# Scores on half the array: a shared PSUM pool, 64-row score matmuls in pairs, and weights cast by DMA

## The chip, the cores and the metric

The kernel runs on one core of one Trainium2 chip. The metric is the device time of one execution in microseconds (us). Five engines of a core work side by side, each through its own queue in order: TensorE (PE, matrix multiply; loading its stationary operand is listed apart as PEld), VectorE (DVE), ScalarE (ACT), GpSimd (POOL) and SyncE (SP, which here only issues DMAs). Matrix products land in PSUM, eight banks of 128 partitions x 512 float32; everything else lives in SBUF, 128 partitions wide. A shape such as 128x448 is partitions x elements per partition.

## The reference

Attention for 8 batches of 12 heads over 448 positions of width 64, then a two-layer feed-forward over all 3584 tokens of width 768. All inputs and the output are float32.

```python
q_n, k_n = (rmsnorm(q, g_q), rmsnorm(k, g_k))      # x / sqrt(mean(x*x) + 1e-6) * g
scores = scale * np.matmul(q_n, k_n.transpose(0, 1, 3, 2))
attn = softmax(scores)
x = matmul(attn, v), heads side by side            # 3584 x 768
h = x @ w_in                                       # 768 x 2048
g = h * np.clip(h + 3.0, 0.0, 6.0) / 6.0
out = g @ w_out                                    # 2048 x 768
```

## The kernel before

**Pairs.** Two heads of one batch make a pair, since two heads of width 64 fill 128 partitions; there are 48 pairs, six per batch. The 448 positions are three blocks of 128 and a rest of 64. For k and v the rest of head 0 and the rest of head 1 are put together in one more block of 128, so a pair has seven key blocks: three of head 0, a mixed one, three of head 1.

**From input to scores.** `load_k`, `load_q` and `load_v` bring two pairs at a time (the first two pairs singly) into staging rings of three groups. `square` (POOL, early also ACT or DVE), `stats_sum` (DVE) and `stats_rstd` (ACT) give 1/rms; `normalize` multiplies it in and rounds to bf16. Then q and k are transposed so that the head width lies on the partitions. For pairs 0 to 13 TensorE does it (`transposes`), and `put_q` and `put_k` copy from PSUM; from pair 14 (`TD`) on a transposing DMA on SP's queue does it (`transposes_dma`), and `scale_q` applies g to q in place. Transposed q has head 0 on partitions 0 to 63 and head 1 on 64 to 127. So that one matmul on all 128 rows gives the scores of a single head, transposed k is kept padded: seven blocks, in which the other head's rows are zero (`clear_k`, `clear_kq`). `put_k` therefore copies in two halves, and the DMA transposes 11 blocks of 128 per pair.

**Scores, softmax, weighing.** `score` is one matmul of 128 rows and 448 columns per key block, into two PSUM banks in turn (`sc_r`). `expo` (ACT) takes the exponential into SBUF. `weigh` multiplies the exponentials by v with a column of ones, so that the row sum comes along; per pair 4 matmuls of 130 columns and 24 of 65, in two halves, into `av_ps` (two banks). `divide` (DVE) normalises, and x is transposed: on TensorE for pairs 0 to 13 (`x_out`, `put_x`), later by a transposing DMA (`x_out_dma`).

**Feed-forward.** `h_mm`: per batch 16 items of six matmuls of 448 columns, followed by `relu` (ACT) and `gate` (DVE). `y_mm`: per block of 128 tokens and half of the output columns, 16 matmuls of 384 columns, then `y_copy` and `y_store`. An item holds one bank from its first matmul to the end of `gate` or `y_copy`. It has three banks (`m_r`), and the two score banks too once all scores are done; the eighth bank (`t_ps`) belongs to the transposes.

**Weights.** Sixteen chunks of 768 KB are loaded by SP into three float32 buffers (`load_w`) and cast to bf16 by whichever of POOL, DVE and ACT the planner picks (`cast_w`). `W_AFTER` says after which group's v load a chunk may be issued.

**What sets the order.** No scheduler of the compiler: `Plan` is a list scheduler that runs while the program is built. Every operation has a key (smaller goes first), the engines that could do it with a planned duration each, and what it depends on. `Plan.run` walks through planned time and emits an instruction when its engine is free. TensorE's feed-forward items stand in two lanes, and a credit (`share`) divides TensorE between them and the attention. The planned durations decide only the order; on the chip every instruction waits for its semaphores.

Of the kernel before, what the change touches and what calls it, by code (L numbers as in the profile page):

```python
# [26 lines left out]
class Op:  # L27

    def __init__(self, key, ways, deps, lag, size):
        self.key, self.ways, self.lag, self.size = key, ways, lag, size
        self.deps = {id(d): d for d in deps if d is not None}
        self.next, self.end, self.time = [], None, 0.0
        for d in self.deps.values():
            d.next.append(self)
        self.left = len(self.deps)


class Item:
    def __init__(self, place):
        self.place, self.ops, self.bank, self.out = place, [], None, None


class Plan:

    HOP = 60
    PRICE, FAIR = {"POOL": 0.5, "ACT": 2.0, "DVE": 1.5}, 0
    ISSUE, LAND, RATE = 600, 1700, 270.0
    STEADY, SLACK = 110e3, 500

    def __init__(self, share):
        self.free = {e: 0.0 for e in ("PE", "ACT", "DVE", "POOL", "SP", "pipe")}
        self.known, self.todo = [], 0
        self.lanes, self.row, self.banks = {"h": [], "y": []}, [], []
        self.share, self.credit = share, 0.0  # L60

    def add(self, key, ways, deps=(), lag=0, size=0, hold=False):
        op = Op(key, ways, deps, lag, size)
# [6 lines left out]
    def dma(self, key, n, size, fn, deps=(), queue="SP", hold=False):  # L70

        return self.add(key, [(queue, self.ISSUE * n, fn)], deps, self.LAND, size, hold)
# [4 lines left out]
    def item(self, lane, place, count, ns, fn, deps):  # L77

        it = Item(place)
        it.ops = [Op(None, [("PE", ns, lambda i=i: fn(i, it.bank[0]))], deps if i == 0 else [], 165, 0)  # L80
                  for i in range(count)]
        self.lanes[lane].append(it)
        return it

    def next_item(self, now, soon):
        best = None
        for lane in self.lanes.values():
            if lane and lane[0].ops[0].left == 0 and (best is None or lane[0].place < best[0].place):
                free = [x for x in self.banks if x[1] is None or x[1].end is not None]
                bank = min(free, key=lambda x: x[1].end if x[1] else 0.0, default=None)  # L90
                if bank is None:
                    continue
                t = max(lane[0].ops[0].time, bank[1].end + self.HOP if bank[1] else 0.0)
                if t <= now:
                    best = (lane[0], bank)
                else:
                    soon.append(t)
        return best

    def begin(self, op, engine, ns, fn, now):  # L100
        fn()
        self.free[engine] = now + ns
        op.end = now + ns + op.lag
        if op.size:
            self.free["pipe"] = max(self.free["pipe"], now + self.ISSUE) + op.size / self.RATE
            op.end = max(op.end, self.free["pipe"] + op.lag)
# [8 lines left out]
    def run(self):  # L115
        now = 0.0
        while self.todo or self.row or any(self.lanes.values()):
            soon = [t for t in self.free.values() if t > now]
            best = {}
            for op in self.known:  # L120
                if op.time > now:
                    soon.append(op.time)
                    continue
                engine, ns, fn = min(op.ways, key=lambda w: max(self.free[w[0]], now) + w[1] * (
                    self.PRICE.get(w[0], 1.0) if op.key[0] >= self.FAIR else 1.0))
                if self.free[engine] <= now and (engine not in best or op.key < best[engine][0].key):
                    best[engine] = (op, ns, fn)
            if self.free["PE"] <= now and ("PE" not in best or self.credit < 0):
                if not self.row:
                    pick = self.next_item(now, soon)  # L130
                    if pick:
                        it, bank = pick
# [3 lines left out]
                        it.bank, bank[1] = bank, it.out  # L136
                        self.row = list(it.ops)
                if self.row:
                    best["PE"] = (self.row[0], *self.row[0].ways[0][1:])
            if not best:  # L140
                now = min(soon)
            for engine, (op, ns, fn) in best.items():
# [10 lines left out]
                self.begin(op, engine, ns, fn, now)  # L153
# [4 lines left out]
def kernel(  # L158
# [25 lines left out]
    NS = 3  # L184
    GP = 2
    NV, NK, NX, NE, NQ = 4, 3, 3, 14, 3
    WC = 256
    WR = 4
    NW = 3
# [16 lines left out]
    q_st = ring(NS, [P, GP, 2, 4, D], FP32, "q_st")  # L206
    k_st = ring(NS, [P, GP, 2, 5, D], FP32, "k_st")
    v_st = ring(NS, [P, GP, 2, 4, D], FP32, "v_st")
    vaug = ring(NV, [P, 4, 2, D + 1], BF16, "vaug")
    kq_r = ring(NK, [P, 11 * P], BF16, "kq")  # L210
    kpad = [x[:, 0:7 * P] for x in kq_r]
    sq_r = ring(2, [P, GP, 8, D], FP32, "sq")
    ssq_r = ring(2, [P, 2, GP, 8], FP32, "ssq")
    lnv_r = ring(2, [P, 2, GP, 8], FP32, "lnv")
    rstd_r = ring(2, [P, 2, GP, 8], FP32, "rstd")
    qk_r = ring(NQ, [P, 2, 4, 2, D], BF16, "qk")
    qT_r = [x[:, 7 * P:7 * P + S] for x in kq_r]
    eT_r = ring(NE, [P, W4], BF16, "eT")
# [4 lines left out]
    w_st = ring(NW, [P, NKT * WC], FP32, "w_st")  # L223

    KQ = 11 * P // 2
    kq_st = [w_st[i][:, 0:KQ].bitcast(BF16) for i in range(NQ)]
# [21 lines left out]
    def part_of(p, n):  # L248
        return (p // GP) % NS, slice(p % GP, p % GP + n)

    def blocks(src):
        return src[:, 0:FULL, :].rearrange("h (p t) d -> p h (t d)", t=NT)

    def load_q(eng, p, n):
        g, pr = part_of(p, n)
        src, dst = heads(q, p, n), q_st[g][:, pr].rearrange("p r h t d -> p (r h) t d")
        eng.dma_start(out=dst[:, :, 0:NT, :].rearrange("p h t d -> p h (t d)"), in_=blocks(src))
# [531 lines left out]
```

## Time and profile before

| | us |
|---|---|
| median of three timed runs | 449.7 (449.42 to 449.94) |
| span of the profiled execution, first to last instruction | 449.5 |
| TensorE busy | 424.5 |
| ACT, DVE, POOL busy | 274.8, 240.1, 229.7 |
| first TensorE matmul starts | 9.9 |
| TensorE busy in the stretch 30 to 60 us | 24.9 of 30 |
| TensorE busy in the stretch 300 to 350 us | 50.0 of 50 |

The page gives no time of its own for the profiled execution beside the span; 0.2 us lie between the span and the median.

How to read it: a line of a group says source line, engine, operation, written tile <- read tiles, shapes and count; then busy time and mean duration in ns; then how long the engine had stood idle just before, and what ended that. Matmuls overlap in the pipeline, so the durations of a group add up to more than the time that passed; the distance between starts is what one costs. The granted clock of TensorE was 0.94 from 30 to 60 us and 1.00 in the other stretches up to 400 us.

### The profile page before, as it was taken

The page shows a single profiled execution, that of the slowest core. Times are in us where ns is not written, and L with a number is a line of the kernel's source. Part 1 is how long each engine was busy: PE and PEld are TensorE (multiplying, and loading weights), DVE is VectorE, ACT ScalarE, POOL GpSimd, SP SyncE. Part 2 cuts the span into 40 slices and gives each one's busy share as a digit, 9 for nine tenths or more (in the row PEclk, how much of TensorE's full clock was granted, in tenths as well). Part 3 has the DMA queues.
Part 4 walks back from the last instruction along what each step waited for, and adds up shares of the span by engine and source line. Part 5 has one row for each costly group of instructions (what it writes and reads, how often), then busy time and mean ns, then how long its engine had stood idle before and what let it go on. Part 6 is the DMA issues. An engine that isn't in the chain of part 4 may idle for free.

```text
span 449.5 us, 9164 instructions
## 1 busy us (share of the span) xinstructions
PE 424.5 (94%) x3512; PEld 255.4 (57%) x3512; DVE 240.1 (53%) x428; ACT 274.8 (61%) x581; POOL 229.7 (51%) x251
## 2 busy tenths in 40 slices
PE   0888799899999989999999999999999999999996
PEld 0455366565566555666566565656565655555563
DVE  6899888845474346646444555453433253343321
ACT  2678678853487678878776777777767551132100
POOL 5899999958577766855667467552310000000000
PEclk9999899999999999999999999999999999999999
DMA  6899999981999999999899777955545210110021
GB/s 160 208 295 247 306 294 283 309 296 47 216 229 191 227 231 199 169 232 188 160 184 219 177 176 171 223 140 76 93 106 72 73 26 36 61 45 36 24 83 70
DMA packets 140908, 73.94 MB, mean 164 GB/s; under 512 B 90176, under 2 KB 137280, under 8 KB 140864
## 3 DMA queue, kind: packets, MB, share of 16 engines
q1 hardware_dynamic: 139232, 72.44, 69.3%
q10 hardware_dynamic: 1632, 0.92, 0.8%
q8 instruction: 27, 0.44, 0.4%
q14 instruction: 17, 0.14, 0.1%
HBM read 45.61 MB, written 11.01 MB: 126 GB/s over the span
## 4 chain that ended last, share of the span: by engine, by line
PE 84%; DMA 6%; POOL 2%; DVE 2%; ACT 2%; SPq 1%; issue 1%; POOLq 0%
PE m L461 29%; PE m L480 26%; PE sc L393 11%; PE av L419 7%; PE sc L480 5%; DMA k_st<-in_k_dram 4%; DMA kq<-w_st 3%; PE sc L461 3%; PE av L413 2%; ACT eT L399 2%; POOL qk L333 1%; POOL sq L315 1%; DVE vaug L280 1%; PE t_ps L349 1%; SPq L277 0%
## 5 line engine op out<-in xcount | busy, mean ns | idle before, releaser
L399 ACT ACTIVATE eT<-sc 128x448 bf16<-128x448 f32 x336 | 175.7, 542 | 48.6 <-PE sc L393 44.6
L461 PE MATMUL m<-xT,w_in_sb 128*128 128x448 bf16 x708 | 165.7, 355 | 0.2
L480 PE MATMUL m<-w_out_sb,gT 128*128 128x384 bf16 x768 | 150.0, 326 | 0.0
L393 PE MATMUL sc<-kq 128*128 128x448 bf16 x336 | 115.9, 359 | 8.2 <-ACT eT L399 6.4
L480 PEld LDWEIGHTS <-gT 128*128 128x128 bf16 x896 | 87.2, 98 | 62.3 <-issue 0.5
L461 PEld LDWEIGHTS <-w_in_sb 128*128 128x128 bf16 x768 | 74.1, 98 | 68.8 <-issue 6.0
L472 DVE SCALAR_TENSOR_TENSOR gT<-t_sb,m 128x448 bf16<-128x448 f32 x118 | 73.0, 620 | 72.9 <-ACT t_sb L467 72.4
L467 ACT ACTIVATE t_sb<-m 128x448 f32<-128x448 f32 x118 | 63.7, 541 | 47.3 <-PE m L461 44.3
L318 DVE TENSOR_REDUCE ssq<-sq 128x16 f32<-128x1024 f32 (+1 forms) x56 | 58.3, 1058 | 8.4 <-POOL sq L315 7.1
L359 POOL TENSOR_TENSOR w_st<-k_st,rstd 128x256 bf16<-128x256 f32 x68 | 40.2, 612 | 41.3 <-DMA kq<-w_st 40.6
L280 DVE COPY y_sb<-m 128x384 f32<-128x384 f32 x39 | 21.7, 557 | 61.4 <-PE m L480 61.2
L419 PE MATMUL av<-vaug,eT 128*128 128x65 bf16 x1152 | 54.5, 194 | 0.0
L419 PEld LDWEIGHTS <-eT 128*128 128x128 bf16 x1152 | 50.8, 99 | 4.4 <-issue 0.4
L315 POOL TENSOR_TENSOR sq<-k_st 128x1024 f32<-128x1024 f32 (+1 forms) x24 | 42.4, 1765 | 12.7 <-DMA k_st<-in_k_dram 5.9
L315 POOL TENSOR_TENSOR sq<-q_st 128x1024 f32<-128x1024 f32 (+1 forms) x26 | 44.5, 1710 | 7.1 <-DMA q_st<-in_q_dram 3.5
L393 PEld LDWEIGHTS <-kq 128*128 128x128 bf16 x336 | 31.3, 99 | 27.0 <-issue 4.9
L413 PE MATMUL av<-vaug,eT 128*128 128x130 bf16 x192 | 42.7, 222 | 0.0
L280 POOL CAST vaug<-v_st 128x512 bf16<-128x512 f32 x29 | 17.9, 618 | 45.2 <-PE av L419 44.6
L367 POOL TENSOR_TENSOR w_st<-q_st,rstd 128x512 bf16<-128x512 f32 x34 | 35.4, 1042 | 0.0
L429 DVE TENSOR_TENSOR xn<-av,rden 128x512 bf16<-128x512 f32 x48 | 33.2, 691 | 1.7
L428 DVE RECIPROCAL rden<-av 128x8 f32<-128x8 f32 x48 | 9.8, 205 | 34.1 <-PE av L419 33.7
L375 ACT ACTIVATE kq<-kq,gprime 128x448 bf16<-128x448 bf16 x34 | 22.6, 663 | 5.1 <-DMA kq<-w_st 5.1
(55 smaller groups left out, 222.5 us busy)
## 6 DMA issues: line engine op xcount, KB each, us to landing
out_dram<-y_sb SPq DMA_DIRECT2D x24, 384.0 KB, 2.9
k_st<-in_k_dram SPq DMA_DIRECT2D x23, 384.0 KB, 4.6
v_st<-in_v_dram SPq DMA_DIRECT2D x23, 384.0 KB, 4.6
q_st<-in_q_dram SPq DMA_DIRECT2D x22, 384.0 KB, 4.7
w_st<-in_moe_w_in_dram SPq DMA_DIRECT2D x8, 768.0 KB, 7.6
w_st<-in_moe_w_out_dram SPq DMA_DIRECT2D x8, 768.0 KB, 7.1
out_dram<-y_sb SPq DMA_DIRECT2D x8, 192.0 KB, 2.7
k_st<-in_k_dram SPq DMA_DIRECT2D x46, 32.0 KB, 3.9
```

What stands on the lines that cost most here:

```text
L280: (eng.copy if eng is nc.scalar else eng.tensor_copy)(out=out, in_=in_)
L315: eng.tensor_tensor(out=sq, in0=x, in1=x, op=A_MULT)
L318: nc.vector.tensor_reduce(out=ssq_r[(p // GP) % 2][:, a, p % GP:p % GP + n, :].rearrange("p r s -> p (r s)"), in_=sq_r[m][:, 0:n].rearrang ...
L359: eng.tensor_tensor(out=blocks[:, c0:c0 + W4].rearrange("p (t c) -> p t c", t=4)[:, :, h * D:(h + 1) * D], in0=raw(0, p, 1)[:, 0, 4 * h:4 ...
L393: nc.tensor.matmul(out=sc_r[n % 2][:, 0:S], lhsT=kpad[p % NK][:, i * P:(i + 1) * P], rhs=qT_r[p % NK], start=True, stop=True,)
L399: nc.scalar.activation(out=eT_r[n % NE][:, 0:S], in_=sc_r[n % 2][:, 0:S], func=EXP, bias=0.0, scale=1.0,)
L413: nc.tensor.matmul(out=av_ps[:, i, 0:2 * W], lhsT=e[3][:, cols], rhs=va[:, 3].rearrange("p h d -> p (h d)"), start=True, stop=False, skip_ ...
L419: nc.tensor.matmul(out=av_ps[:, i, h * W:(h + 1) * W], lhsT=e[4 * h + t][:, cols], rhs=va[:, t, h], start=False, stop=(t == NT - 1 and h = ...
L461: nc.tensor.matmul(out=m[:, 0:S], lhsT=w_in_sb[:, kt, f * P:(f + 1) * P], rhs=xT[:, kt, b % NX, x_slot(b)], start=(kt == 0), stop=(kt == N ...
L467: nc.scalar.activation(out=t[:], in_=m[:, 0:S], func=RELU, bias=0.5, scale=1.0 / 6.0,)
L472: nc.vector.scalar_tensor_tensor(out=gT[:, f, (b % 2) * S:(b % 2 + 1) * S], in0=t[:], scalar=1.0, in1=m[:, 0:S], op0=A_MIN, op1=A_MULT,)
L480: nc.tensor.matmul(out=m[:, 0:n], lhsT=gT[:, f, c0:c0 + P], rhs=w_out_sb[:, f, c:c + n], start=(f == 0), stop=(f == NFT - 1),)
```

## The change

1. **PSUM.** The score banks, the feed-forward banks and the transposes' bank become one pool of six (`bank_r`). An operation names the banks it may use (`want`), and the planner gives it one when the last users have ended. Scores use 0 to 3, the feed-forward and TensorE's transposes 4 and 5; after the last score the feed-forward may use all six.
2. **Scores.** k is no longer padded: `qkT_r` holds k (512 columns) and q. For an unmixed key block `score` issues two matmuls of 64 rows, head 0 on partitions 0 to 63 and head 1 on 64 to 127, into two banks. The program names them as tiles of 64 x 128 at rows 0 and 64 of the array. The mixed block stays one matmul of 128 rows. Up to pair 7 the four steps of a pair are four operations; from pair 8 on two double steps (four half matmuls) stand in one operation, over two pairs as (p: 0, 1), (p: 2; p+1: 0), (p+1: 1, 2). `weigh` is four operations per pair, one per step.
3. **Weights.** Twelve chunks (eight of w_in, four larger ones of w_out) are loaded by DMAs on POOL's queue that write bf16 at once. `cast_w`, the float32 buffers and `clear_kq` go away.
4. **Around these.** `normalize` serves all pairs, `put_k` is one copy of 128 partitions, x is transposed by DMA from pair 6 on (before: 14), staging holds eight single pairs, rings of normalised q and k hold four pairs (before: three), squares are on POOL, up to pair 7 also on ACT. The g vectors are loaded on ACT's queue. Planned durations are other numbers.

```diff
-    sc_r = ring(2, [P, 512], FP32, "sc", psum)
-    m_r = ring(3, [P, 512], FP32, "m", psum)
+    bank_r = ring(3, [P, 2, 512], FP32, "ps", psum)
     av_ps = psum.tile([P, 4, 256], FP32, name="av")
-    t_ps = psum.tile([P, 2, 4 * P], BF16, name="t_ps")
...
-        nc.sync.dma_start(out=dst, in_=src)
+            out, src = w_in_sb[:, :, cols], moe_w_in[:, cols]
...
+        nc.gpsimd.dma_start(out=out, in_=src)
-    def cast_w(eng, n):
...
-    def put_k(p, part):
-        kp = kpad[p % NK]
-        rows, c0 = ((lo, 0), (hi, NT * P))[part]
-        nc.vector.tensor_copy(out=kp[rows, c0:c0 + 4 * P], in_=t_ps[rows, 0, :])
+    def put_k(eng, p, b):
+        copy(eng, out=qkT_r[p % NK][:, 0], in_=bank16(b)[:, 0:W4])
...
-    def score(p, i, n):
-        nc.tensor.matmul(
-            out=sc_r[n % 2][:, 0:S], lhsT=kpad[p % NK][:, i * P:(i + 1) * P],
-            rhs=qT_r[p % NK], start=True, stop=True,
-        )
+    def score(p, i, b):
+        qkT = qkT_r[p % NK]
+        for h, rows in enumerate((lo, hi) if i < NT else (slice(0, P),)):
+            nc.tensor.matmul(
+                out=bank(b[h])[:, 0:S], lhsT=qkT[rows, 0, i * P:(i + 1) * P], rhs=qkT[rows, 1, 0:S],
+                start=True, stop=True,
+            )
...
-        if p >= TD:
+        if p >= HP:
             xo.append(plan.dma_transpose((p + 2, 0), 2 * P * W4, lambda: x_out_dma(p), [div[p]] + late))
...
-    W_AFTER = (2, 2, 2, 2, 3, 3, 3, 3, 4, 4, 5, 5, 6, 6, 7, 7)
+    W_AFTER = (2, 2, 3, 3, 4, 4, 5, 5, 6, 6, 7, 7)
+    w_ops = [plan.dma((-1, n), 1, P * 12288 * 4 // 8 if n < NWI else P * 12288 // 2, lambda n=n: load_w(n),
+                      queue="POOL", hold=True, issue=1000) for n in range(len(W_AFTER))]
...
+    ff_banks = [(4,), (5,)]
...
+    SC = [(0, 1), (2, 3)]
...
+        def steps(todo, pairs=None):
...
+            ns = sum(189 for _ in todo) + (202 if half[0] else 0)
...
+            def run():
+                for n, (p, i) in enumerate(todo):
+                    cells[n]["b"] = cell["b"][2 * n:2 * n + 2]
+                    score(p, i, cells[n]["b"])
...
+            want = (0, 1, 2, 3) if len(todo) == 2 else None
...
+            PB = 8
+        if p < PB:
+            for i in (NT, 0, 1, 2):
+                steps([(p, i)])
+        elif p % 2 == 0:
+            steps([(p, NT)])
+            steps([(p, 0), (p, 1)])
+        else:
+            steps([(p - 1, 2), (p, 0)])
+            steps([(p, NT)])
+            steps([(p, 1), (p, 2)])
...
+    final.ways[0] = (*final.ways[0][:2], lambda: (run_final(), ff_banks.extend([(b,) for b in range(4)])))
```

More of the change, by code (lines that the diff above doesn't have):

```diff
@@ new lines, in weigh @@
+        for j in range(4):
+            c0 = j * P if (p // HP) % 2 == 0 else (j * P - P if j else S - P)
+            for h in range(2 if i < NT else 1):
+                if i == NT:
+                    out, rhs = av_ps[:, j, 0:2 * W], va[:, NT].rearrange("p h d -> p (h d)")
+                else:
+                    out, rhs = av_ps[:, j, h * W:(h + 1) * W], va[:, i, h]
+                nc.tensor.matmul(
+                    out=out, lhsT=e_tile(p, i, h)[:, c0:c0 + P], rhs=rhs,
+                    start=first and j % 2 == 0 and h == 0, stop=last, skip_group_check=True,
+                )
```

620 lines of the change are left out of this document (288 added, 332 removed).

## The prediction

> **What bounds the kernel now.** I read the page first for who is busy, then the busy time by stretch of the span, then TensorE's groups and waits, then the chain that ended last, and at the end the single instructions, for their spacing.
>
> ```profile
> PE 424.5 (94%) x3512; PEld 255.4 (57%) x3512; DVE 240.1 (53%) x428; ACT 274.8 (61%) x581; POOL 229.7 (51%) x251
> ```
>
> ```profile
> 30.00:60.00 30.00, 24.90 (x261) 14.59 (x259) 27.27 (x46) 22.09 (x50) 28.76 (x23) 0.94 1.04 283
> 60.00:100.00 40.00, 38.64 (x382) 24.17 (x380) 30.77 (x57) 30.85 (x67) 33.38 (x26) 1.00 1.06 308
> 100.00:150.00 50.00, 49.76 (x383) 30.04 (x382) 26.76 (x45) 29.43 (x63) 36.22 (x39) 1.00 0.82 170
> ...
> 300.00:350.00 50.00, 50.00 (x418) 30.16 (x415) 18.43 (x34) 36.52 (x73) 12.04 (x18) 1.00 0.51 89
> 350.00:400.00 50.00, 50.00 (x352) 29.06 (x351) 19.39 (x34) 18.66 (x36) 0.00 (x0) 1.00 0.14 41
> ```
>
> The columns are the stretch, its length, then the busy time of PE, weight load, DVE, ACT and POOL, the granted clock, the DMA share and GB/s. From 100 us on TensorE never lets go: the end is the sum of its work. Before that it is fed too slowly: from 30 to 60 us POOL is busy 28.76 of 30 us, DVE 27.27, and the DMA engines are full.
>
> ```profile
> L393 PE MATMUL sc<-kq 128*128 128x448 bf16 x336 | 115.9, 359 | 8.2 <-ACT eT L399 6.4 <-DVE kq L390 1.0
> L413 PE MATMUL av<-vaug,eT 128*128 128x130 bf16 x192 | 42.7, 222 | 0.0
> ```
>
> ```profile
> 399.48 2.60 PE sc L480 x16
> 402.07 1.14 PE sc L461 x6
> ```
>
> A matmul lasts 0.359 us but they overlap, so what counts is the spacing. From the chain: six first-layer matmuls (448 columns) take 1.14 us, 0.189 each; sixteen second-layer ones (384 columns) 2.60, 0.1625 each. The timeline has 0.25 us for one column block of the weighing (one matmul of 130, six of 65 columns), so 1.0 per pair, and 0.055 per transpose. TensorE's work is then 768 x 0.189 = 145.2, 896 x 0.1625 = 145.6, scores 336 x 0.189 = 63.5, weighing 48 x 1.0 = 48.0, transposes 168 x 0.055 = 9.2: 411.5 us. The other 38.0 us of the span are 9.9 before the first matmul, 3.7 after the last, and about 24 of stalls, nearly all ahead of 100 us.
>
> The profiled execution spans 449.5 us, and the median of the three timed runs is 449.7; I sum against the span and add the 0.2.
>
> **The change part by part.**
>
> *Scores.* A pair had seven score matmuls of 448 columns. Now the unmixed key blocks are six matmuls on 64 rows, two at a time on the two halves of the array and into two banks, and the mixed block stays one full matmul. If the halves run at once a pair takes 1 + 3 slots of 0.189 in place of 7: 48 x 3 x 0.189 = 27.2 us less. Against this stands the change between 128 and 64 rows, once in and once out of each uninterrupted group of half matmuls. There are 8 x 3 = 24 such groups in the first eight pairs and 3 per two pairs, so 60, in the other forty: 84. The trace of before holds no 64-row matmul. The lower end is 0. The upper end is that the matmul in flight must come out before the mode changes, at both borders: a matmul outlives its slot by 0.355 - 0.189 = 0.166 us, so 0.332 per group and 27.9 us in all, the whole gain. I take the exposed weight load at both borders, since weights are otherwise loaded beside a running matmul: 98 ns (the weight-load rows) twice, 0.196 x 84 = +16.5 us; it lies between the ends and is the nearest row to what cannot overlap across such a border. Net -10.7.
>
> The Trainium skill, TensorEngine Tiling, Key Properties, says that changing the tiling mode drains TensorE, while tiles of one mode work in parallel. No run here shows either yet; by that rule at its harshest the group costs 0.332 and the sum below becomes 452.4 instead of 441.
>
> *x transposes.* Pairs 6 to 13 go from TensorE (4 x 0.055 = 0.22 each) to SP's transposing DMA: -1.8 us of TensorE. SP gets 8 x 1.23 us of issue, and loses sixteen weight issues of about 0.54: nothing, since SP from 100 us on mostly waits for others.
>
> *Start.* The instruction order of the new program puts the three v loads of pair 0 ahead of the first k load on SP, and the four g loads ahead of the first q load on ACT. In the trace three such issues take from 0.75 to 2.52 us, 1.8; four g issues 2.6. Pair 0's squares, ACT's at 0.63 before, are now POOL's at 1.04. The first transposes start at 9.9 us now; bounds for the delay 0 and 3.1, I take the 1.8 of the k loads, because k is what the first square waits for. +1.8.
>
> *Weights.* Sixteen fp32 chunks were loaded by SP and cast by POOL, 16 x 1.47 = 23.4 us, all between 32 and 101 us, where POOL is nearly full. Now twelve DMAs issued by POOL cast on the way. The trace has no POOL-issued DMA. Lower end 0.54 (SP's issue of the same chunk), upper end 7.6 (issue to landing, if POOL were held all along); I take twice SP's, 1.1, since it is the nearest row, so POOL wins about 10 us in the crowded stretch. DVE wins there too: k goes from two half copies of 0.417 to one of full height. What reaches TensorE is less, because between 30 and 100 us the DMA engines stand at 1.04 and 1.06 of their time: -2, bounds -6 and 0. ACT's 336 exponentials stay, at 175.7 us in all, covered by TensorE.
>
> *Banks.* The feed-forward had three banks of its own; now it shares two with the transposes until the scores are done, and six after. A first-layer bank is held, after its last matmul, by the relu (0.54) and the gate (0.62) with their hand-offs, about 1.5 us; the next item covers 6 x 0.189 = 1.13 of it. Attention left per batch, 6 x (4 x 0.189 + 1.0), is 10.5 us over some 30 items, 0.35 each, and a second-layer item covers 2.6. So two banks just do on the mean, and stalls come where first-layer items follow each other. Lower end 0, upper end 0.4 for the half of some 100 items that follow one of their kind, 20. I take 4, near the lower end: in the trace no matmul of either layer waits for a bank. The four score banks hand over two tiles at a time, where before TensorE waited 6.4 us for exponentials; with more depth I leave this at 0.
>
> Sum: -27.2 + 16.5 - 1.8 + 1.8 - 2 + 4 = -8.7, so 440.8 + 0.2 = 441 us.
>
> **The rivals.**
>
> *The border is cheap.* At 0.1 us per group the sum is 8.1 lower, 433; at 0, 424.5. For it: weight loads mostly hide now, PEld is at 57%. Against it: two loads and a change of shape stand at each border.
>
> *The border drains.* At 0.332 per group, 452.4. It decides from 0.30 on (441 plus 84 x 0.10 is 449.4). If the halves did not overlap at all, the 27.2 would be gone too: 468. That would also be the case in which the change does not do what it says. For it: the 0.166 that a matmul outlives its slot; against it: that end is modelled, and a switch may need only part of it.
>
> *POOL is held by its DMAs.* At 1.95 us per DMA the relief is gone (443); beyond it each microsecond lies on POOL's own work, which feeds the normalised q and k of batches 0 and 1. With all of it exposed, 2.5 us per DMA brings 449.5 and 3.1 brings 457. For it: POOL is at 28.76 of 30 us there; against it: sixteen casts leave, and POOL has four normalised pairs of room. The Trainium skill, SBUF — State Buffer, Who interferes with whom, adds that DVE in its two-port mode locks POOL out while it writes descriptors; no run here shows it yet.
>
> *Two banks are too few.* Ten instead of 4: 447; the full 20: 457. For it: the 1.5 against 1.13; against it: the second layer between.
>
> **How the numbers follow.** Forecast 441 (own range 436 to 447): 0.46. Cheap border: 0.14. Draining border: 0.19, 0.03 of it for halves that do not overlap. POOL held: 0.13. Two banks: 0.08, divided between both sides. Faster 0.46 + 0.14 + 0.03 = 0.63; within 0.2% (0.9 us, about what the three runs, 0.5 apart, can tell) 0.04; slower 0.33. From 431 to 456 the range leaves out half of the cheap case, the missing overlap and a good half of the POOL case, 0.17 together.
>
> **What will show it.** Two half matmuls that start together, and the next group's start 0.19 after a double step plus the border: 84 such borders give its price. First transposes near 11.7 us. POOL without the casts, with twelve issues near 1 us. TensorE's waits: none on DVE's gate if two banks do. A border over 0.3 us, POOL issues over 2.5, or gate waits over 12 us make the forecast wrong.

## The result, and the profile after

The changed kernel takes 601.1 us (597.1 to 604.5, four runs), the kernel before 449.6 beside it: a ratio of 1.336, 95% interval 1.329 to 1.342. The forecast was 441. The profiled execution spans 599.6 us. Times below are medians; a ratio is an estimate of its own, with its interval, and can differ a little from the quotient of two medians. Ratios are of runs in the chip's faster state; one of the four runs of e5_sp_weights was in the slower one, and its median of 465.6 us still counts it (464.3 without).

The page's busy times of the changed kernel:

```profile
PE 443.8 (74%) x3480; PEld 235.5 (39%) x3480; DVE 219.1 (37%) x385; ACT 279.0 (47%) x633; POOL 210.4 (35%) x208
```

No engine has become the bound. TensorE is the busiest still, with 74% in place of 94%. Its busy time by stretch (columns as before: stretch, length, PE, weight load, DVE, ACT, POOL, granted clock, DMA share, GB/s):

```profile
30.00:60.00 30.00, 23.20 (x243) 13.91 (x243) 16.50 (x32) 22.44 (x52) 23.18 (x21) 0.89 1.28 229
60.00:100.00 40.00, 25.42 (x220) 13.21 (x219) 19.21 (x31) 22.02 (x55) 27.07 (x22) 0.96 1.10 219
...
300.00:350.00 50.00, 38.72 (x325) 20.21 (x324) 13.63 (x25) 26.82 (x57) 12.69 (x15) 1.00 0.25 56
350.00:400.00 50.00, 35.20 (x284) 17.77 (x283) 12.07 (x22) 25.49 (x53) 1.24 (x2) 1.00 0.15 35
450.00:500.00 50.00, 38.03 (x202) 19.41 (x201) 13.29 (x23) 8.15 (x15) 0.00 (x0) 1.00 0.07 24
```

Before, TensorE was busy 48.7 to 50.0 of 50 us in every stretch from 100 to 400 us. Now it is busy 35 to 41 of 50 us from 100 us on, even from 450 us on, where only the feed-forward is left, POOL is done and the DMAs rest. No load and no score is left there to explain it. The groups of instructions, with the idle time ahead of them and what ended it, point to a place:

```profile
L411 PE MATMUL ps<-xT,w_in_sb 128*128 128x448 bf16 x768 | 189.5, 354 | 98.7 <-DVE gT L422 42.0 <-ACT t_sb L417 38.4 <-DVE y_sb L282 11.0
L430 PE MATMUL ps<-w_out_sb,gT 128*128 128x384 bf16 x896 | 171.8, 326 | 33.2 <-DVE gT L422 13.9 <-ACT t_sb L417 10.3 <-DVE y_sb L282 9.0
```

Both layers of the feed-forward (L411 and L430, `h_mm` and `y_mm`) wait 132 us for the gate (L422), the relu (L417) and the copy of y (L282): the readers of the feed-forward's banks. The same groups had waited 0.2 and 0.0 us before. And the timeline shows where in an item they wait:

```profile
480.95 1.67 PE L411 MATMUL ps<-xT,w_in_sb 128*128 128x448 bf16 x8 [0.15 <-DVE gT L422]
482.72 0.54 ACT L417 ACTIVATE t_sb<-ps 128x448 f32<-128x448 f32 x1 [1.28 <-PE ps L411]
483.32 0.73 PE L411 MATMUL ps<-xT,w_in_sb 128*128 128x448 bf16 x3 [0.69 <-ACT t_sb L417]
484.15 0.62 DVE L422 SCALAR_TENSOR_TENSOR gT<-t_sb,ps 128x448 bf16<-128x448 f32 x1 [2.06 <-PE ps L411]
484.83 1.49 PE L411 MATMUL ps<-xT,w_in_sb 128*128 128x448 bf16 x7 [0.78 <-DVE gT L422]
```

An item is six matmuls. If two banks were merely too few, TensorE would wait ahead of an item's first matmul. Here eight run, then the next waits for a relu, three run, then the next waits for a gate: these two stops fall inside an item that already has its bank. In the program the eight are an item of six in bank 5 and the first two matmuls of an item in bank 4. Of the latter the first waits for nothing, the third for ACT's relu on bank 5 and the sixth for DVE's gate on bank 5. Matched with the program in this way, 110 of the 132 us lie ahead of a matmul that is not the first of its item. Banks 4 and 5 are the two halves of one tile, `ps2`, since `bank_r` is a ring of three tiles of two banks. The dependencies are set per tile: a write to one half waits for readers of the other half that were emitted ahead of it. The reader waits likewise: the gate stood 2.06 us for a matmul of the other item.

What the prediction forecast of TensorE's own work did come about. Worked out from the starts of all matmuls in the trace: the time before the first one; the spacing of the work; the borders between 128-row and 64-row matmuls; and the standing, that is what is left of the gaps, split at 100 us. Standing so counted includes what matmuls take longer while the granted clock is lower, and the split between it and the borders is good to about 1 us. The rest to the span's end is about 4 us each.

| | first | work | borders | standing to 100 us | after 100 us | span |
|---|---|---|---|---|---|---|
| before | 9.9 | 410.7 | 0 | 22.2 | 2.8 | 449.5 |
| after | 11.2 | 381.7 | 16.2 | 38.2 | 147.9 | 599.6 |

Work and borders fell by 12.8 us. Standing rose by 161.

### The profile page after: what moved, and what is told of

Same layout as the page of the kernel before. It is cut to its first block, busy times and chain, and to the rows that moved or that the text cites. A ratio compares the mean times of both kernels' runs of the same rounds, so it can differ in the third digit from the quotient of the medians.

```text
span 599.6 us, 9120 instructions
## 1 busy us (share of the span) xinstructions
PE 443.8 (74%) x3480; PEld 235.5 (39%) x3480; DVE 219.1 (37%) x385; ACT 279.0 (47%) x633; POOL 210.4 (35%) x208
## 4 chain that ended last, share of the span: by engine, by line
PE 62%; DVE 15%; ACT 13%; issue 4%; DMA 4%; SPq 0%; POOL 0%; DVEq 0%; ACTq 0%; POOLq 0%
PE ps L411 26%; PE ps L430 26%; DVE gT L422 11%; ACT t_sb L417 9%; PE av L378 5%; PE ps L354 5%; DVE y_sb L282 4%; DMA qk_st<-in_q_dram 3%; ACT eD L363 3%; PE ps L331 1%; DMA gq_t<-in_g_q_dram 0%; DVE ssq L305 0%; ACT y_sb L282 0%; DVE qkT L345 0%; DVE qkT L282 0%
## 5 line engine op out<-in xcount | busy, mean ns | idle before, releaser
L411 PE MATMUL ps<-xT,w_in_sb 128*128 128x448 bf16 x768 | 189.5, 354 | 98.7 <-DVE gT L422 42.0
L430 PE MATMUL ps<-w_out_sb,gT 128*128 128x384 bf16 x896 | 171.8, 326 | 33.2 <-DVE gT L422 13.9
L417 ACT ACTIVATE t_sb<-ps 128x448 f32<-128x448 f32 x128 | 69.5, 543 | 202.7 <-PE ps L411 180.6
L422 DVE SCALAR_TENSOR_TENSOR gT<-t_sb,ps 128x448 bf16<-128x448 f32 x128 | 79.2, 621 | 214.2 <-PE ps L411 107.1
L363 ACT ACTIVATE eD<-ps 128x448 bf16<-128x448 f32 x288 | 137.0, 548 | 33.4 <-PE ps L354 33.3
L411 PEld LDWEIGHTS <-w_in_sb 128*128 128x128 bf16 x768 | 72.3, 97 | 148.4 <-issue 105.2
L430 PEld LDWEIGHTS <-gT 128*128 128x128 bf16 x896 | 84.4, 98 | 100.4 <-issue 53.5
L315 POOL TENSOR_TENSOR qkn<-qk_st,rstd 128x512 bf16<-128x512 f32 x96 | 97.6, 1042 | 16.8 <-DMA qkT<-qkn 12.6
L302 POOL TENSOR_TENSOR sq<-qk_st 128x1024 f32<-128x1024 f32 (+1 forms) x47 | 82.8, 1766 | 30.5 <-DVE ssq L305 14.1
L378 PEld LDWEIGHTS <-eD 128*128 128x128 bf16 x1152 | 52.4, 98 | 38.7 <-issue 22.4
L282 DVE COPY y_sb<-ps 128x384 f32<-128x384 f32 x51 | 28.4, 557 | 103.0 <-PE ps L430 71.8
L354 PE MATMUL ps<-qkT 64*128 64x448 bf16 (+1 forms) x336 | 61.4, 367 | 3.5 <-ACT eD L363 1.9
L378 PE MATMUL av<-vaug,eD 128*128 128x65 bf16 x1152 | 60.0, 195 | 0.6 <-ACT eD L363 0.6
L282 POOL CAST vaug<-v_st 128x512 bf16<-128x512 f32 x30 | 18.5, 619 | 112.2 <-PE av L378 93.9
L378 PEld LDWEIGHTS <-eR 128*128 128x128 bf16 x192 | 14.4, 99 | 13.2 <-issue 7.4
## 6 DMA issues: line engine op xcount, KB each, us to landing
w_in_sb<-in_moe_w_in_dram POOLq DMA_DIRECT2D x8, 384.0 KB, 11.1
w_out_sb<-in_moe_w_out_dram POOLq DMA_DIRECT2D x4, 768.0 KB, 16.3
```

The lines of the kernel that those rows point to most:

```text
L282: (eng.copy if eng is nc.scalar else eng.tensor_copy)(out=out, in_=in_)
L302: eng.tensor_tensor(out=sq, in0=x, in1=x, op=A_MULT)
L315: eng.tensor_tensor(out=qkn_r[p % NQ][:, a].rearrange("p t h d -> p h t d"), in0=qk_st[:, a, p % NS], in1=rstd_r[p % NR][:, a].rearrange(" ...
L354: nc.tensor.matmul(out=bank(b[h])[:, 0:S], lhsT=qkT[rows, 0, i * P:(i + 1) * P], rhs=qkT[rows, 1, 0:S], start=True, stop=True,)
L363: nc.scalar.activation(out=e_tile(p, i, h)[:, 0:S], in_=bank(b[h])[:, 0:S], func=EXP, bias=0.0, scale=1.0,)
L378: nc.tensor.matmul(out=out, lhsT=e_tile(p, i, h)[:, c0:c0 + P], rhs=rhs, start=first and j % 2 == 0 and h == 0, stop=last, skip_group_chec ...
```

## The experiments

### One tile per bank

Two banks per tile is one line of the change. **e1_six_tiles** changes it alone:

```diff
-    bank_r = ring(3, [P, 2, 512], FP32, "ps", psum)
+    bank_r = ring(6, [P, 512], FP32, "ps", psum)
...
-        return bank_r[b // 2][:, b % 2]
+        return bank_r[b][:]
```

> The six banks become six tiles of one bank each, in place of three tiles of two; order, banks and work stay the same. Theory (waits set by the tile): in the trace of the changed kernel a feed-forward matmul into one bank stops in the middle of its item for the relu and the gate that read the other bank of the same tile; TensorE is 37 to 41 us busy of 50 even where only the feed-forward is left. With one bank per tile these waits go and the time is my forecast's sum, 441 us (436 to 447). Rival, two banks are too few: the same two banks serve, so the time stays above 560. Rival, POOL is held by its DMAs, or the DMAs are late: nothing of that changes, above 560. Rival, the border between 64 and 128 rows is dear: also unchanged, above 560.

Measured: 470.4 us (469.7 to 472.3), 1.042 [1.036, 1.048] of before. The same groups:

```profile
L411 PE MATMUL ps<-xT,w_in_sb 128*128 128x448 bf16 x768 | 174.6, 356 | 8.7 <-DVE gT L422 8.5
L430 PE MATMUL ps<-w_out_sb,gT 128*128 128x384 bf16 x896 | 167.5, 327 | 3.2 <-DVE gT L422 3.2
```

The 132 us have become 12, and the time fell by 131. Instructions, banks and their users are the same, so two feed-forward banks were not too few; they were not two for the waits. The rivals had all expected more than 560. But the time is 29 us above the forecast's sum, so a second cause is left.

**e3_ff_tiles** takes only the two feed-forward banks apart and leaves the score banks in two tiles of two:

```diff
-    bank_r = ring(3, [P, 2, 512], FP32, "ps", psum)
+    bank_r = ring(2, [P, 2, 512], FP32, "ps", psum) + ring(2, [P, 512], FP32, "ff", psum)
...
-        return bank_r[b // 2][:, b % 2]
+        return bank_r[b // 2][:, b % 2] if b < 4 else bank_r[b - 2][:]
```

> As the changed kernel, but banks 4 and 5 (feed-forward and TensorE's transposes) are tiles of their own, while the score banks stay two tiles of two banks. Theory: if the feed-forward's banks carry the loss, within 10 us of the six-tile version, 441 to 455; the score banks only matter where two single steps follow and in the tail, where the feed-forward may use them. If the score banks carry half of it, about 520.

Measured: 469.1 us, 1.038 [1.032, 1.045]. As e1 within the uncertainty. The score tiles of two banks cost nothing measurable; that a step writes both banks of a tile together would account for it, but no run tests that.

**e2_before_shared** does the harm alone, to the kernel before. Two of its three feed-forward banks become one tile:

```diff
-    m_r = ring(3, [P, 512], FP32, "m", psum)
+    m_two = psum.tile([P, 2, 512], FP32, name="m_two")
+    m_r = [m_two[:, 0], m_two[:, 1], psum.tile([P, 512], FP32, name="m2")]
```

> The kernel before, with two of its three feed-forward banks put into one tile of two banks and nothing else changed. Theory (waits set by the tile): items that follow each other in these two banks now stop for each other's relu and gate; in the changed kernel that cost about 150 us over 184 items, 0.8 each, here it is a part of the items: 490 to 560 us. Rivals (banks too few, POOL's DMAs, the border): this kernel has none of these, so 449.6.

Measured: 503.4 us, 1.114 [1.107, 1.121]. TensorE's waits in it (engine, line, waited for; us in total, times, longest):

```profile
PE m_two L462 <- DVE gT L473: 13.1, 23, 0.8
PE m_two L462 <- ACT t_sb L468: 12.3, 21, 0.7
```

The same two waits appear in a kernel that has nothing else of the change, and it takes 52 us more, with the third bank still a tile of its own. The first cause is shown in both directions.

### The double steps

What is left, 470 against 451.6 of before in the same comparison, stands in e1's matmul starts as: work 381.7, borders 15.8, standing 35.8 to 100 us and 20.1 after. **e4_single_steps** is e1 without double steps, one step of two half matmuls at a time throughout:

```diff
-            PB = 8
+            PB = NPAIR
```

> Six single-bank tiles, and every 64-row step alone up to the last pair (no two steps in one go). Groups of half matmuls go from 84 to 144. At the border that I took (0.196 us in and out) this costs 60 x 0.196 = 11.8 us against the six-tile version; a cheap border (0.1) gives 6, one that drains both ways (0.332) gives 20. If the halves did not overlap there would be no difference in slots, and the border alone would show.

Measured: 478.1 us, 1.059 [1.054, 1.064]. Borders 28.3 us in place of 15.8, standing 50.9 in place of 55.9; the difference of the two, 7.5, is the 7.7 measured. At the borders the double steps save 12.5 us, near the 11.8 of the prediction's price; 5.0 of it comes back as standing. The borders are not what holds e1 above before: e1's work and borders together are 13.2 us below before's.

### The weights on POOL's queue

**e5_sp_weights** takes e1's weights back to SP and the casts to the engines, as before. The float32 buffers need room, so staging shrinks from eight pairs to six and the normalised ring from four to three; **e8_small_rings** is the control, e1 with the small rings alone. **e6_before_pool_weights** puts the change's weight DMAs, alone, into the kernel before. **e7_late_w_out** is e1 with the four w_out chunks, half of the weights' bytes, two groups later.

```diff
-    NS = 8
-    NV, NK, NX, NQ, NR = 4, 3, 3, 4, 4
+    NS = 6
+    NV, NK, NX, NQ, NR = 4, 3, 3, 3, 4
```

That was e8; e5 has it too, takes w_out in eight chunks of half the size, and has

```diff
-        nc.gpsimd.dma_start(out=out, in_=src)
...
+        nc.sync.dma_start(out=dst, in_=src)
...
+    def cast_w(eng, n):
...
-    W_AFTER = (2, 2, 3, 3, 4, 4, 5, 5, 6, 6, 7, 7)
+    W_AFTER = (2, 2, 2, 2, 3, 3, 3, 3, 4, 4, 5, 5, 6, 6, 7, 7)
```

e6 is the reverse of this in the kernel before, and e7 reads

```diff
-    W_AFTER = (2, 2, 3, 3, 4, 4, 5, 5, 6, 6, 7, 7)
+    W_AFTER = (2, 2, 3, 3, 4, 4, 5, 5, 8, 8, 9, 9)
```

> Six single-bank tiles, and the weights as in the kernel before: sixteen float32 chunks on SP's queue, cast by the engines; staging of six pairs and rings of three pairs as before, so that it fits. Theory (crowded loads): in the six-tile version q and v loads of 50 to 67 us land after 12.8 and 13.4 us, beside weight chunks of POOL's queue that land after 8.8 to 19.4; the late loads hold the in-order queues and TensorE starves between 60 and 150 us. Without POOL's DMAs most of the 29 us between 470 and my sum go: 440 to 452. Rival (two banks or the order of the front): the weights are innocent, 465 to 475, or more for the casts.

> The control for the version with weights on SP: six single-bank tiles, weights by POOL's DMAs, staging of six pairs and rings of three pairs. Both theories: near the six-tile version's 470, 466 to 478.

> The kernel before with only the weights changed: twelve casting DMAs on POOL's queue after the groups that the changed kernel uses, no casts by engines. Theory (crowded loads): slower, since two queues now share the DMA engines in the stretch where they are full: 458 to 475. Rival (the weights are innocent): POOL is relieved of 23.4 us of casts, 445 to 451.

> Six single-bank tiles, and the four w_out chunks asked for after the v loads of groups 8, 8, 9 and 9 in place of 6, 6, 7 and 7. Theory (crowded loads): the q and v loads of 50 to 75 us land sooner, 455 to 465, if the second layer is not kept waiting for its weights. Rival: unchanged, 468 to 472, or slower where the weights come too late.

Measured, with before at 450.6:

| | us | ratio to before |
|---|---|---|
| e8_small_rings | 475.0 | 1.054 [1.049, 1.059] |
| e5_sp_weights | 465.6 (464.3) | 1.026 [1.020, 1.032] |
| e6_before_pool_weights | 455.0 | 1.010 [1.007, 1.012] |
| e7_late_w_out | 468.8 | 1.039 [1.037, 1.043] |

From e8 to e5, taking the weights off POOL's queue gains 9 us by the medians and 12.5 by the ratios; putting them there costs 4.5 us in the kernel before, where the prediction gave the step a gain of 2. Loading w_out later is worth nothing measurable. Crowded loads do not come out as the main part: e7 lies where its rival had it, e5 at the lower edge of its rival's bounds and 13 us above those of the theory, and e6 between the bounds of both. What the DMAs do to the other loads can be read off the q loads that start between 15 and 100 us, from issue to landing. The kernel before, and then e6 with POOL's weights alone:

```profile
DMA to landing us min/median/max: 4.2/5.7/8.6
```

```profile
DMA to landing us min/median/max: 4.0/7.7/13.0
```

The loads of k and v go the same way there, from a median of 6.3 to 8.7 and of 6.2 to 8.2 us. And e1, then e5, where the weights are back on SP:

```profile
DMA to landing us min/median/max: 3.7/8.8/13.8
```

```profile
DMA to landing us min/median/max: 3.8/5.7/6.7
```

On one queue the weights stood in line with the loads. On a second they run beside them, and the loads take longer while they do. That fits the 4.5 us of e6 and a part of what e5 gains, but landing times alone do not set the time: in e7 the q loads' median is down to 6.3 us, and the time did not follow. e5 still takes 12 to 15 us more than before, so it is not all.

### Loads that come later than the order expects

e1's timeline in the stretch of its worst standing (start, length, engine, line, operation; in brackets the idle time before and what ended it):

```profile
60.10 0.55 PE L354 MATMUL ps<-qkT 64*128 64x448 bf16 x4
60.84 1.48 PE L411 MATMUL ps<-xT,w_in_sb 128*128 128x448 bf16 x7
63.58 1.89 POOL L302 TENSOR_TENSOR sq<-qk_st 128x1024 f32<-128x1024 f32 x1 [7.37 <-DMA qk_st<-in_q_dram]
65.50 1.22 DVE L305 TENSOR_REDUCE ssq<-sq 128x16 f32<-128x1024 f32 x1 [5.64 <-POOL sq L302]
66.76 0.22 ACT L311 ACTIVATE lnv<-ssq 128x16 f32<-128x16 f32 x1 [6.27 <-DVE ssq L305]
67.19 0.53 ACT L363 ACTIVATE eD<-ps 128x448 bf16<-128x448 f32 x1
67.77 0.24 PE L378 MATMUL av<-vaug,eD 128*128 128x65 bf16 x1 [5.44 <-ACT eD L363]
```

A q load lands late. POOL waits for it with a square, DVE with that square's sum, ACT with that sum's logarithm. The scores of the step at 60.10 were ready for their exponentials by 60.7, but these stand behind the logarithm in ACT's queue until 67.2, and TensorE, which needs them, stands 5.44 us. Over the stretch from 55 to 150 us POOL waits 14.9 us in this way, DVE 18.1 and ACT 12.6.

The queues run in the order that `Plan` wrote down, and `Plan` believes that loads move at 270 bytes per ns, at half of that while SP's stream and POOL's are both under way, and that a w_out chunk is half its float32 size. Four kernels of one comparison (before at 451.1) separate two theories. A: the transfers are crowded, and what the change moved into them must come out. B: the loads are out of step with the order written down. **e9_x_tensor** is e1 with the x transposes of pairs 6 to 13 back on TensorE; **e10_plan_loads** is e1 with only the plan's numbers changed; **e11_both** has both; **e12_sp_x** is e5 with e9's edit.

```diff
-        if p >= HP:
+        if p >= TD:
             xo.append(plan.dma_transpose((p + 2, 0), 2 * P * W4, lambda: x_out_dma(p), [div[p]] + late))
```

```diff
-    ISSUE, LAND, RATE = 600, 1700, 270.0
+    ISSUE, LAND, RATE = 600, 1700, 200.0
...
-    w_ops = [plan.dma((-1, n), 1, P * 12288 * 4 // 8 if n < NWI else P * 12288 // 2, lambda n=n: load_w(n),
+    w_ops = [plan.dma((-1, n), 1, P * 12288 * 4 // 8 if n < NWI else P * 12288, lambda n=n: load_w(n),
```

> The six-tile kernel (470.4 us, TensorE standing 18.7 us between 60 and 100 us and 11.6 between 100 and 150) with one thing more undone: the x transposes of pairs 6 to 13 go back to TensorE, as before, so the sync queue carries 34 DMA transposes of xT and not 42 while the loads of q, k and v run late. Theory A (a crowded transfer system up to 110 us delays the loads, and the transposes by DMA are part of the crowd): 462 to 466 us, and POOL's squares wait for the q loads under 10 us between 55 and 150 us (14.9 now). Theory B (the loads are late against the order written out, whoever crowds them): within 2 us of 470.4, plus or minus the 32 TensorE transposes, 1.8 us.

> The six-tile kernel with only the planner's view of the loads changed: 200 bytes per ns for each of the two streams in place of 270, and the w_out chunks at their full float32 bytes (twice what the plan has). The same instructions run, in another order. Theory B (the written order puts squares, sums and the logarithm of a late pair in front of ready exps and gates on POOL, DVE and ACT): the waits of DVE for POOL's squares and of ACT for the sums (18.1 and 12.6 us between 55 and 150 us) fall to a half or less and the time to 455 to 463. Theory A (the loads themselves are too late, whatever the order): 467 to 473, the wait only moves.

> Both of the two edits: x transposes of pairs 6 to 13 on TensorE, and the slower loads in the plan. If the two causes add: 450 to 458. If they are one cause seen twice: as the better of the two alone, within 2 us.

> The six-tile kernel with the weights loaded by the sync queue and cast on the engines (465.6 us) and the x transposes of pairs 6 to 13 on TensorE. Then all that the change moved into the transfers is back where it was; what is left of it is the shared pool of six tiles, the 64-row scores and the unpadded k. Theory A (crowded transfers cause all of the 31 us of standing over the kernel before): 440 to 452. Theory B: 458 to 466, the order still set by loads that the plan has too early.

| | us | ratio to before |
|---|---|---|
| e9_x_tensor | 464.4 | 1.030 [1.025, 1.035] |
| e10_plan_loads | 454.4 | 1.006 [1.002, 1.010] |
| e11_both | 452.2 | 1.002 [0.999, 1.006] |
| e12_sp_x | 451.8 | 1.003 [1.000, 1.006] |

e10 runs the very same instructions as e1 in another order and takes 16 us less, a little more than theory B gave it; A allowed 3. But e9 came out where A had it (though POOL's wait for q loads fell only to 12.8 us and not under 10), and e12, which leaves the plan's rate alone and clears the transfers, reached the same place as e11, at the upper end of A's bounds and 6 us below B's. The edits of e9 and e10 gain 6.0 and 16.0 alone and 18.2 together, less than their sum, so in part they are two ways to one thing. Nor did the waits that e10 was to halve fall so far: 13.5 us of DVE on POOL's squares (18.1 in e1) and 14.3 of ACT on the sums (12.6). TensorE's standing fell all the same, from 55.9 to 39.2 us, most of it after 100 us (20.1 to 7.2). In e11 one late load is left between 60 and 100 us, and its timeline shows a second way from a load to TensorE:

```profile
79.31 1.50 PE L411 MATMUL ps<-xT,w_in_sb 128*128 128x448 bf16 x7
81.17 3.74 POOL L302 TENSOR_TENSOR sq<-qk_st 128x1024 f32<-128x1024 f32 x2 [5.66 <-DMA qk_st<-in_q_dram]
83.10 1.22 DVE L305 TENSOR_REDUCE ssq<-sq 128x16 f32<-128x1024 f32 x1 [4.82 <-POOL sq L302]
84.24 0.20 DVE L386 RECIPROCAL rden<-av 128x8 f32<-128x8 f32 x1
84.47 0.69 DVE L387 TENSOR_TENSOR xn<-av,rden 128x512 bf16<-128x512 f32 x1
85.21 0.59 PE L378 MATMUL av<-vaug,eR 128*128 128x130 bf16 x4 [4.41 <-DVE xn L387]
86.20 1.14 DVE L422 SCALAR_TENSOR_TENSOR gT<-t_sb,ps 128x448 bf16<-128x448 f32 x2
...
88.68 2.69 PE L411 MATMUL ps<-xT,w_in_sb 128*128 128x448 bf16 x8
```

The square of a later pair waits 5.66 us for its q. DVE's next instruction is that square's sum, and behind it stand the division of a pair whose weighing is done and the gates of finished items. Only then do they run, one after the other, and TensorE, which needed the division, has stood 4.41 us.

Three runs with before at 450.6 ask what holds 452 above 437, which is before's 450.6 less the 13.2 us that e1 has less of work and borders. B again: **e13_sp_x_plan** is e12 with the plan's rate at 220, **e14_both_slower** e11 at 160. A: **e15_both_late** is e11 with e7's late w_out. C: neither, but the pool itself.

```diff
-    ISSUE, LAND, RATE = 600, 1700, 270.0
+    ISSUE, LAND, RATE = 600, 1700, 220.0
```

> Weights by the sync queue, x transposes of pairs 6 to 13 on TensorE, and the plan's load rate at 220 bytes per ns (the kernel without the last edit took 451.8 us, with 8.6 us of standing between 60 and 100 us and 9.8 between 150 and 250). Theory B (what is left is still loads that the plan has too early): standing between 60 and 100 us falls to 4 or less and the time to 444 to 448, under the kernel before. Rival C (what is left is the pool of two banks and the engines' order, whatever the loads do): 450 to 453.

> The kernel with both edits (weights cast by POOL's transfers, x transposes on TensorE, load rate 200 in the plan: 452.2 us, one stand of 4.4 us at 81 us behind a q load that came 5.7 us after its plan) with the rate at 160. Theory B: that stand goes, 446 to 449. Rival C: 451 to 454, since a plan that expects loads too late starts other work too late.

> The same kernel at rate 200 with the four w_out chunks behind the loads of pair groups 8, 8, 9 and 9 in place of 6, 6, 7 and 7, so that 6.3 MB come about 30 us later than now. Theory A (crowded transfers make the one late q load): the stand at 81 us goes, 446 to 449. Rival C: 451 to 454; or 455 and more if the first y items come to wait for w_out.

Measured: e13 461.3 us, 1.026 [1.023, 1.029]; e14 469.9, 1.044 [1.041, 1.047]; e15 452.9, 1.005 [1.003, 1.007]. e15 lies in the bounds of C, the other two in none. A slower rate in the plan, which gained 16 us between 270 and 200 in e1, costs 10 from 270 to 220 with the weights on SP and 18 from 200 to 160 with them on POOL. In e14 the standing to 100 us did fall (28.5 in e11, 23.9 here), as B says, but after 100 us it rose from 5.7 to 29.4: that fits the reason in C's line, a plan that expects loads too late starts other work too late, but C allowed 2 us for it, and the time rose by 18.

The last three (before at 450.6) look at that number from the other side, **e17_sp_x_300** with e12 at 310 and **e18_both_230** with e11 at 230, and ask whether the two causes add: **e16_two_bank_tiles** is the changed kernel, tiles of two banks and all, with e11's two edits.

> The changed kernel, its pool of three tiles of two banks kept, with only the two edits that bring the loads and the order together (x transposes of pairs 6 to 13 on TensorE, load rate 200 and the w_out chunks at their full bytes). If the two causes are separate and add, it stays 130 us above the same kernel with six tiles (452.2): 578 to 590, and nearly nothing of the long standing beyond 150 us goes. If the standing on tiles and the late loads are one thing, it comes below 540.

> Weights by the sync queue, x transposes of pairs 6 to 13 on TensorE, and the plan's load rate at 310 bytes per ns, where 270 gave 451.8 us and 220 gave 461.3. If the time falls with a plan nearer to the rate of this stage (before moves 308 GB/s between 60 and 100 us): 444 to 449. If 270 stands near the best, or the rate only shuffles the order: 451 to 462.

> Weights cast by POOL's transfers, x transposes on TensorE, w_out at its full bytes in the plan, load rate 230, where 200 gave 452.2 us and 160 gave 469.9. If the time has one smooth minimum in the rate, it lies near 200 to 230: 447 to 452. If the rate only shuffles the order: anything between 450 and 465.

Measured: e16 639.5 us, 1.414 [1.403, 1.426]; e17 457.5, 1.012 [1.004, 1.020]; e18 454.0, 1.008 [1.006, 1.010].

So over the rate: 469.9 at 160, 452.2 at 200, 454.0 at 230 with the weights on POOL; 461.3 at 220, 451.8 at 270, 457.5 at 310 with them on SP. Each series is best at the middle one of its three points, and neither comes under the kernel before. Whether the best rate goes with what the transfers move is not shown: from 60 to 100 us that is 231 GB/s in e11 and 279 in e12, yet 230 was not better than 200, and e17 and e18 both lie where a rate that only shuffles the order would put them. And the two causes do not add as expected: the two edits that take 18 us from the six-tile kernel add 38 to the two-bank one, where two separate causes would have given 578 to 590 and one cause less than 540. There TensorE's x transposes of eight more pairs use banks 4 and 5, so they are more users of the one tile that everyone waits for, and the order is another:

```profile
PE ps L411 <- ACT t_sb L417: 43.1, 71, 1.2
PE ps L411 <- DVE gT L422: 42.1, 62, 1.8
PE ps L430 <- DVE gT L422: 17.6, 28, 1.2
```

These waits alone do not make 38 us more than the changed kernel's (38.4, 42.0 and 13.9). The granted clock has a part: leaving out the end, it is 0.50 for 37 us in e16 and for 17 in the changed kernel, which by these figures is worth 10 us at most. How the rest comes about was not followed further.

## Why the prediction was wrong, step by step

- **Scores, -27.2: right.** Work fell by 29.0 us, which is the 27.2 and the 1.8 of the x transposes. A double step, four half matmuls, shows in the changed kernel's timeline as one stretch of 0.55 us, which is one matmul of 0.355 and one slot of 0.196; single starts of two halves lie 3 ns apart.

```profile
301.58 0.55 PE L354 MATMUL ps<-qkT 64*128 64x448 bf16 x4
307.39 0.55 PE L354 MATMUL ps<-qkT 64*128 64x448 bf16 x4
```

- **Border, +16.5: right.** 16.2 us: 0.096 into the 64-row mode and 0.093 out of it, 0.189 per group against the 0.196 taken, in 80 groups, not 84, since some groups came to stand side by side. At 0.189 these would be 15.1 us; after a single step the way out takes 0.103, and at some borders TensorE took longer still. That is about the length of a weight load twice (98 ns), the price that the step took; that the weight loads are the reason is not shown. Both rivals on the border fall. The Trainium skill, TensorEngine Tiling (Array Packing), Key Properties, is borne out in that tiles of one mode run together; of the drain the trace shows these 0.19 us, not the 0.332 of a matmul's full tail.
- **Start, +1.8: nearly right.** First matmul at 11.2, not 11.7 us.
- **Weights, -2: the sign was wrong.** The price of the issue was right:

```profile
L294 POOL DMA_DIRECT2D w_in_sb<-in_moe_w_in_dram x8: 824/854/1005, 22.9 to 45.6; - x8
L294 POOL DMA_DIRECT2D w_out_sb<-in_moe_w_out_dram x4: 881/910/937, 50.4 to 64.4; - x4
```

0.85 and 0.91 us each against 1.1, and the rival in which POOL is held falls. But the step said itself that the DMA engines were full from 30 to 100 us, and then counted only POOL's relief. In the kernel before the step alone costs 4.5 us, and the loads of q, k and v land later.

- **Banks, +4: the step that failed.** It costed the banks as a matter of how many there are: how long an item holds one and what covers that. With six tiles this is right within its bounds: the waits of both layers for the gate are 8.5 and 3.2 us, just under the 12 that the prediction set as its limit, and 5.5 of the 8.5 are a single wait in which the gate itself stood behind a late q load. In e11 they are 2.7 and 1.4, the 4 that the step took. What it passed over, and so put at nothing, is that the diff makes one tile of two banks: both layers then wait 132 us, and one bank per tile takes 131 us off the time. It took "in the trace no matmul of either layer waits for a bank" as a reason for the low end, although that row belongs to banks that were each a tile of their own. The upper end of 20 came from the same model, and so held nothing of the 131 us. The rival "two banks are too few" named the right place and the right wait, for another reason, and its highest price, 20 us, is less than a sixth of what the step cost.
- **What the sum did not have.** It took the standing as before, apart from the terms. e1 stands 31 us more than before, 22 of which e11 takes away. An estimate: about 5 of the 31 are the clock, since it is granted at 0.50 for 17.0 us in e1, in which TensorE is busy 12.8, and for 3.4 in before, busy 3.3, and half of that work's time is what the lower clock adds. The sum treated the time to 100 us as TensorE's to save, but 14 pairs are divided by 100 us in before, 14 in e11, 12 in e1 (counting the reciprocals): there, it seems, the loads set the pace, and a TensorE with less to do stands longer. What e11 lacks at 100 us is feed-forward: 108 first-layer matmuls against 126 and none of the second layer against 19, which is 18 x 0.189 + 19 x 0.1625 = 6.5 us.

With one bank per tile and both of e11's edits, the balance of e11's profile against before's is: work and borders -11.2, first matmul +1.3, standing +9.2, which makes the 0.7 by which its span (448.8) is shorter. The timed median is 452.2 against 451.1 for before in its comparison, so even that is not a gain. No kernel here beats the kernel before. What stays open is how the 18 us divide between crowded transfers and the order: every edit of the one also changes the other, since the order is planned anew each time, and a new rate alone moved the time by 2 to 18 us. Whether some order reaches 437 was not found.

## What to carry to other kernels

When a diff regroups buffers, look at what the waits are set on: in this program two banks in one tile are one buffer for the dependencies, and the sign of it in a trace is an engine that stops in the middle of an accumulation for the readers of its neighbour. A wait that the trace of before does not show says nothing about a buffer that the change builds anew. And where in-order queues are written by a planner, a load that moves from one queue to another is a change of every queue: change the planner's numbers with it, and read the queue behind the first late load before costing an engine's relief as a gain.

## What the runs showed of the hardware

- A change between 128-row and 64-row matmuls costs 0.096 us one way and, in the changed kernel, 0.093 the other after a double step and 0.103 after a single one (medians). e4, nearly all of it single steps, has the same 0.096 and 0.103, and its 140 groups cost 28.3 us in all.
- After a longer stand TensorE runs slower for a while. In e11's timeline above, after 4.41 us without work, eight first-layer matmuls take 2.69 us, where eight take 1.67 in the changed kernel's timeline; the granted clock is 0.50 there from 83.9 to 90.7 us. For e1 from 60 to 100 us, with its stands of up to 5.5 us, it is 0.83:

```profile
60.00:100.00 40.00, 27.16 (x237) 14.47 (x237) 18.21 (x31) 21.95 (x56) 28.30 (x24) 0.83 1.13 218
```

  The Trainium skill, TensorE: Matmul & The Clock Gate, Part 1, puts the drop to half rate at one idle window of about 3.4 us. e11's drop comes 3.1 us into its stand, which is near that, but so long a stand was not needed here: the changed kernel's clock falls to 0.50 at 120.9 us after 3.4 us (117.5 to 120.9) in which TensorE was busy for 1.60 and no stand was longer than 0.78, and e1's at 104.9 us after 3.4 in which it was busy for 1.30. From 150 to 598 us, with TensorE busy 35 to 41 of 50 us, the changed kernel keeps 1.00. Many short stands close together can thus lower the clock too.
- Weight DMAs that cast on the way take a median of 11.1 us (w_in) and 16.3 us (w_out) from issue to landing in the changed kernel, and hold POOL for 0.82 to 1.01 us each.
